# RWKV-5 attention into a cosine router: the order of the lead-in on GpSimd and ScalarE, of the embeddings' transposes, and of the first early transposes

## The chip, the cores and the metric

The kernel runs on one core of a Trainium2 chip. The metric is the time of one execution on the device in microseconds (us), as a median over several executions. Engines are named as in the profile: PE is TensorE's matrix unit, PEld its weight loads, DVE VectorE, ACT ScalarE, POOL GpSimd, SP the SyncE queue that issues most DMAs.

## What is computed

The reference chains two blocks. The first is an RWKV-5 linear attention over 4 batches, 8 heads, 768 steps and 48 channels per head. The second routes each of the 3072 resulting rows of 384 numbers to one of 8 experts by a cosine score, and applies that expert.

```python
for t in range(S):                                     # attention, per batch b and head h
    cur = einsum('bhd,bhe->bhde', u * k[t], v[t])
    y[t] = einsum('bhd,bhde->bhe', r[t], state + cur)
    state = w * state + einsum('bhd,bhe->bhde', k[t], v[t])
x = y.transpose(0, 2, 1, 3).reshape(3072, 384)
logits = normalised(x) @ normalised(expert_emb).T / tau
expert = argmax(logits); gate = softmax(logits)[expert]
out[row] = gate * (relu(x[row] @ w1[expert]) @ w2[expert])
```

## The kernel before

Everything is fp32. Attention is done in chunks of 128 steps: 6 chunks by 4 batches make 24 units, and unit n is chunk n // 4 of batch n % 4. After it come the experts, one after the other, sorted by how many rows they got. No scheduler moves anything: on every engine the instructions stand in the order in which the Python code issues them, and each engine works through its own queue in that order. Order in the code is therefore the subject of this case.

**What a unit needs.** The keys `K` and receptances `R` of a unit are loaded as 128 steps by 8 heads by 48 channels. `scaled` (L317) multiplies K by `kpow`, powers of the decay w, into one of four padded tiles `Kpad`. `turn_r` (L360, L362) transposes R on PE and multiplies it by the decay powers `rpow` into `RT`. `turn_k` (L369, L378) transposes Kpad on PE into the PSUM tile `kt` and copies it on ACT into `KT`. `scores` (L388) multiplies KT by RT into two PSUM tiles `at`; `masked` (L394) applies the triangular mask on DVE, into `AT0` and `AT1`. `sums` (L443, L452) multiplies the old state and the values V by these into `y`, copied on ACT to `yT` (L457). `states` (L409) computes what the chunk adds to the state, `carry` (L422 to L425) adds it. The term with u is taken apart: `own_k` and `own_r` (L328, L332, both on POOL) make u·k·r in the tile `KU`, `own_sum` (L337) adds it up on DVE into `diag`, and `own_rows` (L346) multiplies V by it on ACT into `xd`. `rows` (L470, L476) transposes yT back on PE and adds xd on DVE into the rows `X`. `turn_rows` (L556, L558) transposes X once more, into the PSUM tile `xp` and, by an ACT copy, into `xT`, which the router's logits (`logits`, L572) use.

**The loop.** `attention` runs i from -1 to 23. An iteration turns R and K of unit i + 1, prepares on POOL Kpad, KU of unit i + 2, finishes `sums` and `states` of unit i, makes scores and masks of unit i + 1, rows of unit i, and the transposes of the rows of unit i - 1. Small steps of the router, of the constants' tables (`build_turned`, L197 to L213) and of the expert embeddings (`build_experts`) are put in between. The embeddings are scaled on ACT (L248), transposed on PE (L252) and copied on DVE into `ent` (L253).

**The lead-in.** `build_first` comes before the loop. It loads unit 0, has DVE make the powers of w (L89 to L95), ACT `rpow` (L98) and then eight small casts of constants (`cast`, L126), transposes `kp` on PE into the PSUM tile `kpT` (L107), and copies that on DVE into `kpow` (L110). Unit 0's own Kpad is multiplied in place from the same PSUM tile (L112). On POOL `own(k, 0)`, that is L328 and then L332, stands before the first `scaled` of the loop, which is unit 1's.

**The way into the experts.** In unit 22 the two least filled experts are already known, and one tile of rows for each is gathered by an indirect DMA (`Early`, L1010). Each has a `turn()` (L1021 on PE into the PSUM tile `early_x`, L1023 on ACT into `earlyx`) and 16 steps on PE, eight `early_h` (L1032) and eight `early_y` (L1041). Behind the loop these steps are dealt out by `fill(n)` between the last routing steps.

**PSUM tiles** are given out by tag from fixed banks in turn. Tag `tp` has banks 0 and 1 and serves rt, yrows, lgT, rank, lists and early_x; tag `xp` has the one bank 7 and serves kpT, xp and the embeddings' ps; tag `st` has bank 6. A tile of a tag waits until the earlier one in that bank has been read.

Of the kernel before, what the change touches and what calls it, by code (L numbers as in the profile page):

```python
# [48 lines left out]
def build_first(k):  # L49


    nc, pool = k.nc, k.aconst
    wc = pool.tile([128, NP], F32, name="wc")
    nc.vector.memset(wc, 1.0)
    with nc.allow_non_contiguous_dma(reason="384 words"):
        for s, q in ((0, nc.sync), (1, nc.scalar)):
            q.dma_start(out=wc[s * DP : s * DP + D, :], in_=k.w.rearrange("(p s) d -> s d p", s=2)[s])
    k.ones = k.const.tile([128, 128], F32, name="ones")
    nc.vector.memset(k.ones, 1.0)
    wide = k.work.tile([128, 512], F32, name="wide", tag="AT1")  # L60
    nc.vector.memset(wide, 1.0)
    k.ident = k.const.tile([128, 128], F32, name="ident")
    make_identity(nc, k.ident)

    def busy(columns):
        ps = k.ps.tile([128, 512], F32, name="wake", tag="y")
        nc.tensor.matmul(ps[:, 0:columns], k.ones, wide[:, 0:columns], start=True, stop=True)

    for _ in range(WAKE):
        busy(512)  # L70
    k.Kpad, k.Rpad = (
        [pool.tile([128, H, DP], F32, name=f"{name}{i}") for i in range(count)]
        for name, count in (("Kpad", 4), ("Rpad", AHEAD + 2))
    )
    pads = k.Kpad + k.Rpad
    for t in pads:
        nc.gpsimd.memset(t[:, :, D:DP], 0.0)
    load(k, 0, k.Kpad[0])
    for i in range(1, AHEAD - 1):
        load(k, i)  # L80
    load_rows(k)


    nc.gpsimd.tensor_scalar(wc, wc, W_MIN, W_MAX, ALU.max, ALU.min)
    build_numbers(k)
    own(k, 0)
    t = pool.tile([128, NP, C], F32, name="wpow")
    for p in range(NP):
        nc.vector.tensor_tensor_scan(  # L89
            t[:, p, :], wc[:, p : p + 1].to_broadcast([128, C]), k.ones, 1.0, ALU.mult, ALU.mult  # L90
        )
    mid = pool.tile([128, NP], F32, name="mid")
    nc.vector.reciprocal(mid, t[:, :, C // 2])
    kp = k.work.tile([128, NP, C], F32, name="kp", tag="AT0")
    nc.vector.tensor_mul(kp, t[:, :, ::-1], mid[:, :, None].to_broadcast([128, NP, C]))  # L95
    k.rpow = pool.tile([128, NP, C], F32, name="rpow")
    for p in range(NP):
        nc.scalar.mul(k.rpow[:, p, :], t[:, p, :], mid[:, p : p + 1])  # L98
    cast(k)

    kt = turned_k(k, 0)
    k.KT[0] = k.work.tile([128, NP, C], F32, name="KT", tag="KT")
    nc.vector.tensor_mul(k.KT[0], kt, kp)
    turn_r(k, 0)
    ps = k.ps.tile([128, NP, 2, DP], F32, name="kpT", tag="xp")
    for p in range(NP):
        nc.tensor.transpose(ps[:, p].rearrange("q s d -> q (s d)"), kp[:, p, :], k.ident)  # L107
    busy(192)
    k.kpow = pool.tile([128, H, D], F32, name="kpow")
    nc.vector.tensor_copy(k.kpow.rearrange("q (p s) d -> q p s d", s=2), ps[:, :, :, 0:D])  # L110
    first = k.Kpad[0].rearrange("q (p s) d -> q p s d", s=2)[:, :, :, 0:D]
    nc.vector.tensor_mul(first, first, ps[:, :, :, 0:D])  # L112
    k.wC = t[:, :, C - 1 : C].to_broadcast([128, NP, D])
# [10 lines left out]
def cast(k):  # L124
    for f, i in k.casts:
        k.nc.scalar.copy(f, i)  # L126
    k.casts.clear()
# [192 lines left out]
def own(k, i):  # L320

    own_k(k, i)
    own_r(k, i)
# [68 lines left out]
def masked(k, i, s):  # L392
    a = k.work.tile([128, NP, C], F32, name=f"AT{s}", tag=f"AT{s}")
    k.nc.vector.tensor_mul(a, k.at[i][s], k.umask[:, None, :].to_broadcast([128, NP, C]))  # L394
    k.AT.setdefault(i, []).append(a)
# [451 lines left out]
def attention(k):  # L847


    units = B * NCH  # L850

    def on(f, i, *more):
        if 0 <= i < units:
            f(k, i, *more)

    def of_group(f, i):
        if 0 <= i < units:
            f(k, k.groups[i // B], i % B)

    def whole(f, i, *more):  # L860
        if 0 <= i < units and i % B == B - 1:
            f(k, k.groups[i // B], *more)

    emb, tables = build_experts(k), build_turned(k)
    for i in range(-1, units):
        j = i - SETTLED * B
        if 0 < i + AHEAD < units:
            load(k, i + AHEAD)
        whole(places, i - 4)
        whole(logits_out, i - 3)  # L870
        if i >= 0:
            on(turn_r, i + 1)
        if i == 0:
            own_sum(k, i)
        if B <= i < units - 1:
            on(own_rows, i, 0)
        if i >= 0:
            on(turn_k, i + 1)
        if 0 < i < B:
            own_rows(k, i, 0)  # L880
        whole(turn_logits, i - 3)
        if i == B + 3:
            norms(k, k.groups[0])
        on(scaled, i + 2)
        on(own, i + 2)
        for n in SQUARES.get(i, (i - 1,)):
            of_group(squares, n)
        if B <= i < units - 1:
            on(own_rows, i, 1)
        if i > B + 1:  # L890
            whole(norms, i - 2)
        if j == 10:
            k.lists = turned_lists(k, perm, "tp")
            lists = taken_by_rank(k, k.lists)
            first = [Early(k, r, *lists, w) for r, w in zip(LAST, k.weights)]
        whole(choose, i - 3)
        whole(before, i - 3)
        whole(located, i - 4)
        whole(gates, i - 5)
        whole(lanes, i - 5)  # L900
        whole(listed, i - 5)
        if 0 <= i < units - 2:
            on(own_sum, i + 1)
        if i == B:
            next(emb)
        if j == 7:
            load_, count = loads(k, "xp")
        if j == 9:
            expert_of(k, by)
            number = expert_number(k, LAST[0])  # L910
            load_w1(k, number, k.weights[0][0])
        on(sums, i)
        on(states, i)
        for n in (0, 1) if i == 0 else (1,) if 0 < i < B else ():
            own_rows(k, i, n)
        whole(taken, i - 6, "xp")
        whole(exps, i - 4)
        on(carry, i)
        if 0 < i < B + 2:
            next(tables)  # L920
        whole(summed, i - 6)
        on(scores, i + 1)
        on(masked, i + 1, 0)
        if i == 0:
            masked(k, i + 1, 1)
        on(rows, i)
        if i != 0:
            on(masked, i + 1, 1)
        if i == units - 2:
            own_sum(k, i + 1)  # L930
            own_rows_once(k, i + 1)
        of_group(put, i)
        if j == 10:
            load_w2(k, number, k.weights[0][1])
        of_group(turn_rows, i - 1)
        whole(logits, i - 2)
        whole(ranks, i - 3)
        if i == 0:
            build_constants(k)
        if i in (1, 2, 3):  # L940
            next(emb)
        if 3 <= i < 3 + len(k.ring):
            k.nc.gpsimd.memset(k.ring[i - 3], 0.0)
        if j == 8:
            by = order(k, load_)
        if j == 9:
            settle(k, by, count)
            perm = turner(k, by)


    g, h = k.groups[NCH - 2], k.groups[NCH - 1]
    early = itertools.chain(*(f.steps(lambda: to) for f in first))

    def fill(count):
        for _ in range(count):
            next(early, None)

    load_weights(k, expert_number(k, LAST[1]), k.weights[1])
    first[0].turn()
    gates(k, g)  # L960
    lanes(k, g)
    listed(k, g)
    turn_rows(k, h, B - 1)
    first[1].turn()
    squares(k, h, B - 1)
    norms(k, h)
    fill(1)
    logits(k, h)
    logits_out(k, h)
    fill(1)  # L970
    turn_logits(k, h)
    choose(k, h)
    before(k, h)
    to = outs(k, lists[0], E * TM)
    taken(k, g, "tp")
    fill(2)
    ranks(k, h)
    load_, _ = loads(k, "xp")
    places(k, h)
    exps(k, h)  # L980
    located(k, h)
    lanes(k, h)
    gates(k, h)
    listed(k, h)
    summed(k, g)
    by = order(k, load_, k.settled)
    perm = turner(k, by)
    fill(6)
    taken(k, h, "tp")
    summed(k, h)  # L990
    fill(1)
    lists = turned_lists(k, perm, "xp")
    k.take, k.gates = taken_by_rank(k, lists)
    k.rows_of = {r: gathers(k, r) for r in LAST}
    k.to = outs(k, k.take, E * TM)
    caps_passed(k, load_, by)
    for _ in early:
        pass
# [615 lines left out]
```

## Time and profile before

| What | us |
|---|---|
| median of 6 runs (lowest, highest) | 400.19 (400.1, 400.63) |
| the profiled execution | 400.13 |
| its span, first to last instruction | 398.0 |
| busy in the span: PE, PEld | 387.6, 352.5 |
| busy in the span: DVE, ACT, POOL | 254.4, 172.7, 161.6 |
| mean granted TensorE clock | 0.995 |

The profiled execution took 400.13 us, of which 2.13 lie outside the span. A row of the timeline is: start in us, busy us, engine, source line, operation, output and inputs, shapes, count of instructions, and in brackets the engine's idle time just before with what ended it. Several instructions of one kind that follow each other are one row. A matmul of fp32 data counts twice, a transpose once.

### The profile page before, as it was taken

To read this page: it belongs to the slowest core of one execution; us is meant where nothing else is said; L and a number is where in the kernel's file an instruction comes from. 1 tells how busy PE (TensorE), PEld (TensorE's weight loads), DVE (VectorE), ACT (ScalarE), POOL (GpSimd) and SP (SyncE) were. 2 spreads that over 40 slices of the span, in tenths; PEclk is the share of its full clock that TensorE was granted. 3 is DMA by queue.
4 is the path that set the end of the run, shared out by engine and by line. 5 is a ranking of instruction groups with operands and counts; after the bars stand their busy time and mean duration, and the time that the engine had idled before them with its cause. 6 is when DMAs were issued, how large, how long until landed. Compare 5 with 4: busy or idle time off the path is not lost.

```text
span 398.0 us, 9267 instructions
## 1 busy us (share of the span) xinstructions
PE 387.6 (97%) x3542; PEld 352.5 (89%) x3542; DVE 254.4 (64%) x601; ACT 172.7 (43%) x523; POOL 161.6 (41%) x216
## 2 busy tenths in 40 slices
PE   7999999999999999999999999999999999999993
PEld 4888888888888777899999999999999999899783
DVE  6887888888788770666667668266365556656601
ACT  3787777767677411433233332233233243133020
POOL 7999696867664232500701502220350350300111
PEclk9999999999999999999999999999999999999998
DMA  7999997767615972243705613334164170150111
GB/s 146 177 187 195 195 202 156 151 134 150 135 42 201 310 270 68 87 161 159 254 4 185 231 72 128 104 140 161 45 235 158 43 226 13 40 179 0 40 39 44
DMA packets 93797, 54.35 MB, mean 137 GB/s; under 512 B 76938, under 2 KB 88381, under 8 KB 93747
## 3 DMA queue, kind: packets, MB, share of 16 engines
q1 hardware_dynamic: 90242, 44.26, 40.9%
q0 software_dynamic: 3296, 9.44, 7.3%
q8 instruction: 29, 0.48, 0.5%
q14 instruction: 22, 0.17, 0.1%
q10 hardware_dynamic: 208, 0.00, 0.0%
HBM read 44.45 MB, written 9.63 MB: 136 GB/s over the span
## 4 chain that ended last, share of the span: by engine, by line
PE 91%; ACT 3%; DVE 1%; POOL 1%; DMA 1%; issue 1%; SPq 0%; POOLq 0%; DVEq 0%
PE ps L1222 25%; PE ps L1286 18%; PE ps L1326 5%; PE at L388 5%; PE y L452 5%; PE ps L1340 4%; PE yrows L470 3%; PE early_h L1032 3%; PE early_y L1041 3%; PE ps L1200 3%; PE rt L360 2%; PE ps L1170 2%; PE y L443 2%; PE kt L369 2%; PE st L409 2%; PE xp L556 2%
## 5 line engine op out<-in xcount | busy, mean ns | idle before, releaser
L1086 POOL DMA_INDIRECT out_dram<-y,to x25 | 30.5, 1221 | 173.1 <-DVE Sh L1361 110.0
L1222 PE MATMUL ps<-xTe,w 128*128 128x192 f32 (+3 forms) x336 | 62.9, 327 | 0.0
L1222 PEld LDWEIGHTS ps<-xTe,w 128*128 128x128 f32 x336 | 55.9, 190 | 0.5
L346 ACT ACTIVATE xd<-V,diag 128x48 f32<-128x48 f32 x184 | 46.2, 325 | 0.0
L394 DVE TENSOR_TENSOR AT<-at,umask 128x512 f32<-128x512 f32 x48 | 32.7, 684 | 9.6 <-PE at L388 9.4
L1229 ACT ACTIVATE hT<-hT 128x384 f32<-128x384 f32 (+3 forms) x42 | 22.0, 523 | 32.6 <-DVE hT L1252 16.7
L1286 PE MATMUL ps<-Tw,Sh 128*128 128x192 f32 x192 | 32.5, 326 | 0.0
L1286 PEld LDWEIGHTS ps<-Tw,Sh 128*128 128x128 f32 x192 | 31.4, 190 | 0.0
L1077 POOL DMA_INDIRECT G<-xs,take x25 | 27.0, 1081 | 10.5 <-issue 5.8
L1222 PE MATMUL ps<-Tx,Sw 128*128 128x192 f32 (+3 forms) x168 | 29.7, 326 | 0.0
L388 PE MATMUL at<-RT,KT 48*128 48x128 f32 x384 | 27.9, 285 | 0.3 <-DVE RT L362 0.3
L1239 DVE TENSOR_TENSOR u<-ps,p 128x384 f32<-128x384 f32 (+3 forms) x14 | 7.8, 558 | 31.4 <-ACT p L1236 16.6
L1222 PEld LDWEIGHTS ps<-Tx,Sw 128*128 128x128 f32 x168 | 27.6, 190 | 0.1
L452 PE MATMUL y<-AT,V 128*48 128x128 f32 (+1 forms) x384 | 26.2, 278 | 0.0
L388 PEld LDWEIGHTS at<-RT,KT 48*128 48x128 f32 x384 | 23.3, 187 | 2.6 <-issue 0.9
L332 POOL TENSOR_TENSOR KU<-KU,Rpad 128x384 f32<-128x384 f32 x24 | 24.2, 1007 | 1.9
L452 PEld LDWEIGHTS y<-AT,V 128*48 128x48 f32 (+1 forms) x384 | 19.8, 124 | 4.4 <-issue 3.4
L1286 PE MATMUL ps<-w,hT 128*128 128x192 f32 x128 | 23.4, 326 | 0.0
L328 POOL TENSOR_TENSOR KU<-K,u_bc 128x384 f32<-128x384 f32 x23 | 23.3, 1011 | 0.0
L317 POOL TENSOR_TENSOR Kpad<-K,kpow 128x384 f32<-128x384 f32 x23 | 23.1, 1006 | 0.1
L558 ACT COPY xT<-xp 128x384 f32<-128x384 f32 x24 | 11.5, 479 | 25.1 <-PE xp L556 23.9
L1249 ACT ACTIVATE hT<-ps 128x384 f32<-128x384 f32 (+3 forms) x14 | 6.9, 491 | 35.5 <-PE ps L1222 32.5
(240 smaller groups left out, 817.9 us busy)
## 6 DMA issues: line engine op xcount, KB each, us to landing
w<-in_moe_w_dram SPq DMA_DIRECT2D x16, 1536.0 KB, 7.0
Rpad<-in_r_dram SPq DMA_DIRECT2D x24, 192.0 KB, 5.1
V<-in_v_dram SPq DMA_DIRECT2D x24, 192.0 KB
xs<-X SPq DMA_DIRECT2D x24, 192.0 KB, 3.0
K<-in_k_dram SPq DMA_DIRECT2D x23, 192.0 KB, 3.5
G<-xs,take POOLq DMA_INDIRECT x27
out_dram<-y,to POOLq DMA_INDIRECT x25
Kpad<-in_k_dram SPq DMA_DIRECT2D x1, 192.0 KB
```

What stands on the lines that cost most here:

```text
L317: k.nc.gpsimd.tensor_mul(k.Kpad[i % len(k.Kpad)][:, :, 0:D], k.loaded[i][0], k.kpow)
L328: k.nc.gpsimd.tensor_mul(k.KU[i], k.loaded[i][0], k.u_bc)
L332: k.nc.gpsimd.tensor_mul(k.KU[i], k.KU[i], k.loaded[i][1][:, :, 0:D])
L346: k.nc.scalar.mul(k.xd[i][:, h, :], V[:, h, :], diag[:, h : h + 1])
L388: nc.tensor.matmul(at[s][:, p, :], KT[rows, p, :], RT[rows, p, :], start=True, stop=True)
L394: k.nc.vector.tensor_mul(a, k.at[i][s], k.umask[:, None, :].to_broadcast([128, NP, C]))
L452: mm(y[s][u * DP : u * DP + n, q, :], V[:, h * D : h * D + n], AT[s][:, p, :], start=(c == 0 and q == 0), stop=True, skip_group_check=True,)
L1077: nc.gpsimd.indirect_dma_start(out=G[0:n, :], out_offset=None, in_=k.xs[:, :], in_offset=IndirectOffsetOnAxis(ap=take[0:n], axis=0), bound ...
L1086: put = k.nc.gpsimd.indirect_dma_start(out=k.out[:, :], out_offset=IndirectOffsetOnAxis(ap=to, axis=0), in_=y, in_offset=None, bounds_chec ...
L1222: nc.tensor.matmul(ps[:, j, :], weights[:, (f + j) * 128 : (f + j + 1) * 128], moving, start=(first and j == 0), stop=True, skip_group_che ...
L1229: nc.scalar.activation(h, h, ACT.Relu)
L1286: nc.tensor.matmul(ps, a[:, f, :], b[:, f, :], start=(first and f == 0), stop=(f == NF // 2 - 1), skip_group_check=True)
```

## The change

Five edits in three places. In the lead-in, `own(k, 0)` is cut in two: `own_k` stays in `build_first`, and `own_r` of unit 0 moves into the loop's first iteration, behind `scaled` of unit 1. The copy of kpT into `kpow` goes from DVE to ACT, in front of the eight casts, which were in front of the transposes. In iteration 4 the last step of the embeddings (three transposes on PE and the copy into `ent` on DVE) moves from in front of `sums` to behind `states`, `carry`, a step of the tables and `summed`. At the end of attention, the first expert's `turn()` moves from behind the loop to in front of `rows` of unit 23; the second one's takes the place of the first, and is followed by a `fill(1)` that is new there.

```diff
@@ build_first
     build_numbers(k)
-    own(k, 0)
+    own_k(k, 0)
...
         nc.scalar.mul(k.rpow[:, p, :], t[:, p, :], mid[:, p : p + 1])
-    cast(k)
...
     k.kpow = pool.tile([128, H, D], F32, name="kpow")
-    nc.vector.tensor_copy(k.kpow.rearrange("q (p s) d -> q p s d", s=2), ps[:, :, :, 0:D])
+    nc.scalar.copy(k.kpow.rearrange("q (p s) d -> q p s d", s=2), ps[:, :, :, 0:D])
+    cast(k)
@@ attention, in the loop
         on(scaled, i + 2)
+        if i < 0:
+            own_r(k, 0)
         on(own, i + 2)
...
-        if i == B:
-            next(emb)
...
         whole(summed, i - 6)
+        if i == B:
+            next(emb)
         on(scores, i + 1)
         on(masked, i + 1, 0)
         if i == 0:
             masked(k, i + 1, 1)
+        if i == units - 1:
+            first[0].turn()
         on(rows, i)
@@ attention, behind the loop
     load_weights(k, expert_number(k, LAST[1]), k.weights[1])
-    first[0].turn()
+    first[1].turn()
+    fill(1)
     gates(k, g)
     lanes(k, g)
     listed(k, g)
     turn_rows(k, h, B - 1)
-    first[1].turn()
     squares(k, h, B - 1)
     norms(k, h)
     fill(1)
```

## The prediction

> **What bounds the kernel now.** I read the page first: PE is busy nearly throughout, so time is won only where PE waits.
>
> ```profile
> PE 387.6 (97%) x3542; PEld 352.5 (89%) x3542; DVE 254.4 (64%) x601; ACT 172.7 (43%) x523; POOL 161.6 (41%) x216
> ```
>
> Then the view of waits, for PE over the whole span. Its columns are the total, the number of times and the longest.
>
> ```profile
> PE kt L369 <- POOL Kpad L317: 0.6, 1, 0.6
> PE rt L360 <- DMA Rpad<-in_r_dram: 0.4, 1, 0.4
> PE xp L556 <- ACT xT L558: 0.4, 1, 0.4
> ...
> PE ps L252 <- ACT emb L248: 0.2, 1, 0.2
> PE yrows L470 <- ACT yT L457: 0.2, 1, 0.2
> ```
>
> The three places of the change are three of these waits: 0.6 for unit 1's kt, 0.2 for the embeddings, 0.2 + 0.4 at the last rows. Together that is 1.2 us, 0.3% of the time, so each must be followed in the timeline. The lead-in first, then the landing of unit 1's K (the view of DMA issues around 4 us; the last column is us from issue to landing):
>
> ```profile
> 7.15 1.00 POOL L328 TENSOR_TENSOR KU<-Kpad,u_bc 128x384 f32<-128x384 f32 x1 [1.59 <-DMA u_bc<-in_u_dram]
> 7.32 0.55 DVE L110 COPY kpow<-kpT 128x384 f32<-128x384 f32 x1
> ...
> 8.23 1.00 POOL L332 TENSOR_TENSOR KU<-KU,Rpad 128x384 f32<-128x384 f32 x1
> ...
> 9.05 0.63 PE L360 MATMUL rt<-ident,Rpad 128*128 128x128 f32 x4 [0.44 <-DMA Rpad<-in_r_dram]
> 9.19 1.00 POOL L317 TENSOR_TENSOR Kpad<-K,kpow 128x384 f32<-128x384 f32 x1
> ...
> 10.24 0.66 PE L369 MATMUL kt<-ident,Kpad 128*128 128x128 f32 x4 [0.56 <-POOL Kpad L317]
> ```
>
> ```profile
> K<-in_k_dram SPq DMA_DIRECT2D x1, 192.0 KB, 4.6
> ```
>
> Unit 1's Kpad stands on POOL behind KU's second multiplication, which nobody needs before DVE's diag at 10.45. Its inputs are there early: K, issued at 3.29, landed at 3.29 + 4.6 = 7.89, and kpow was ready at 7.87.
>
> **The lead-in, term by term.** POOL: L328 ends at 8.15, so Kpad runs from 8.19 to 9.19 and KU's L332 after it, to 10.19. The same three operations fill the same stretch, so POOL is where it was from 10.14 on. diag still finds its KU at 10.45.
>
> kpow: DVE loses 0.55. ACT gains a copy of 128x384 from PSUM, the shape of xT, whose row at 18.32 says 0.48. kpT is complete at 6.21 + 0.60 = 6.81 and ACT's rpow ends at 6.60, so kpow is there at about 7.35 and Kpad's start at 8.19 has 0.8 to spare. The eight casts slide from 6.50 to 7.34 and end at about 8.4. Behind them stands ACT's KT copy, which waited 3.33 for PE, so the 0.84 is hidden; without that cover it would cost just that. DVE's free time is worth nothing: its next step, L112, waits until 8.18 for L328 to have read Kpad.
>
> PE: rt stays at 9.05, held by its load. A kt that need not wait starts 0.15 before the rt row ends (13.82 + 0.60 against 14.27), so unit 1's starts at 9.68 - 0.15 = 9.53 with Kpad done at 9.19: 0.71 earlier. It also takes 0.60 instead of 0.66, which makes 0.77 at most. I take 0.74. Next in PE's queue is unit 0's `y`, now at about 10.08. Its masks end at 9.31 and 9.93. V's landing is not in these rows; K landed at 7.89 and R by 9.05, one load in some 1.1, so I estimate V at 10.0 to 10.2, and what it may cost at 0 to 0.1.
>
> **Does the 0.74 pass on?** PE runs without a gap from 10.82 to 27.7, so it does unless another engine, which has not moved, comes to stand in the way. POOL is such a one: its rows follow each other without idle time from 7.15 to 35.20. Cover left after PE moves up by 0.74 (row minus what it needs):
> - kt of units 2, 3, 4 behind Kpad: 13.53 - 13.18, 17.82 - 17.43, 22.12 - 21.97 = 0.35, 0.39, 0.15.
> - RT of unit 2: DVE waits for POOL's KU until 12.26, so its copy of the state stays at 12.73 and the masks behind it move by only 0.43, from 13.48 to 13.05. RT ends at 15.83 - 0.43 = 15.40; the scores want it at 16.26 - 0.74 = 15.52. Cover 0.12.
> - diag of units 3 and 4 (19.82, 24.23) can move by only 0.3 and 0.15, as KU ends at 19.49 and 24.03. The masks behind diag 3 have more cover than that. Unit 4's, finished at 28.11, are wanted by the second half of `y` at about 28.1 after the shift and the move of the embeddings; should PE stand there a little, the wait for ACT below covers it.
>
> The covers are thin but all positive. In iteration 4 the lead passes to ACT:
>
> ```profile
> 25.25 1.20 DVE L206 TENSOR_SCALAR mask<-number,own 128x8 f32<-128x8 f32 x1
> ...
> 26.92 0.48 ACT L558 COPY xT<-xp 128x384 f32<-128x384 f32 x1 [0.44 <-PE xp L556]
> ...
> 31.11 0.61 ACT L457 COPY yT<-y 112x256 f32<-112x256 f32 x2
> 31.50 0.46 PEld L470 LDWEIGHTS yrows<-ident,yT 112*128 112x128 f32 x4 [0.26 <-ACT yT L457]
> ```
>
> ACT works without a gap from xT at 26.92 to yT at 31.11, and yrows waits for it. But that stretch begins with a wait for PE's xp, so it moves up with PE. From 36.6 on PE is bound again and the rest follows it: 0.74 at the end.
>
> The mask row is odd: 1.20 us for 8 columns where the tie of the same shape (L213, at 35.85) took 0.17. It ended at 26.45, with POOL's KU (25.42 to 26.43). DVE now meets an unmoved POOL at other moments, so such a hold can come or go; by this row it is worth up to 1.03 of DVE. The scores are masked from 26.37 on, after it, and the covers above leave room even for an unmoved mask, so I count 0, between 0 and 0.2.
>
> [...]
>
> **The embeddings.** Three transposes (0.35) with their wait (0.20) leave the place before unit 4's `y` and go behind its states; ent (0.17 on DVE) goes with them. PE reaches `y` about 0.5 earlier, but the yrows that follow at 31.50 wait for ACT's queue, not for y (done at 29.90). Moved up, the transposes still fit before them: the next scores end at 31.43 in the old order. ent is wanted by lgT at 37.57, and the next xp at 32.02 shares its bank, both far off. Value 0, bounds +0.3 (the transposes in front of the scores, uncovered) and -0.2 (their wait gone).
>
> **The last rows.** All times here are before the 0.74.
>
> ```profile
> 132.09 0.41 PE L470 MATMUL yrows<-ident,yT 112*128 112x112 f32 x2 [0.19 <-ACT yT L457]
> ...
> 132.66 0.49 PE L1021 MATMUL early_x<-ident,G 128*128 128x128 f32 x3
> ...
> 132.92 0.23 ACT L646 ACTIVATE l<-l 128x32 f32<-128x32 f32 x1 [0.89 <-DVE l L645]
> 133.06 0.46 ACT L558 COPY xT<-xp 128x384 f32<-128x384 f32 x1
> ...
> 133.57 0.55 PE L556 MATMUL xp<-ident,X 128*128 128x128 f32 x3 [0.42 <-ACT xT L558]
> ```
>
> early_x in front of yrows fills the 0.19. The 0.42 looks open to filling too, but its cause stays. ACT stands at the exp until 132.92, for DVE. In the old order the copy after it frees bank 7 for xp. In the new one earlyx's copy comes first, and PE's next step is the second early_x, which needs that bank of tag `tp` back: yrows sits in the other. So PE again goes on at about 133.57, having done the same work. From there both orders hold the same set up to the logits' transpose, one early_h moved. The xp that follows now comes at about 134.7, behind an xT copy that ends at 134.0; lgT's fourth matmul wants the last xT at 135.8, which is ready at 135.7. Value 0, bounds -0.6 (both waits gone) and +0.2.
>
> The new `fill(1)` puts the routing chain one early_h (0.77, from 134.28 to 135.05) later; the gathers at 145.98 to 150.00 feed PE only at 158.79. No DMA moves in SP's or POOL's queue.
>
> **Sum.** The profiled execution is 398.0 of span and 2.13 around it: 400.13 - 0.74 = 399.39, against a median before of 400.19. I say 399.4. A measurement of this kernel can tell about 0.2%, 0.80 us, from no change; the border, 399.39, runs through my forecast.
>
> **Rivals.**
> - *POOL holds the units back.* For it: the covers of 0.12 and 0.15. Against it: they are positive. If one cover is short by 0.4, 0.3 remains: 399.8. Chance 0.13.
> - *Nothing comes of it*: K lands later than 9.2 in the new order, or ACT's stretch from 26.92 does not move up. K's 7.89 and ACT's wait for xp speak against it. 400.1, chance 0.05.
> - *The pauses at the last rows go as well*: 0.74 + 0.61 = 1.35, so 398.8. For it: PE's order is freer. Against it: the shared bank. Chance 0.14.
> - *Slower: early_x waits for its gather.* PE works in order, so with early_x in front, yrows, xp and the routing stand behind the gather's landing. The gather is issued by 127.92; packets of its queue still run between 131.5 and 132.0, and PE asks at 131.56. ACT takes the result only at 133.06, so early_x, 0.49 long, may start as late as 132.5 for nothing; beyond that each us costs one, and 1.3 later than now it decides the sign. Behind a 1536 KB load, at the 390 GB/s of 125 to 129 us some 3.9, it would be 400.13 - 0.74 + 3.4 = 402.8. Against it: the next such load is issued at 130.79, after the gather. Chance 0.08.
>
> **Chances and range.** Forecast 0.60 (399.2 to 399.6, of which 0.36 past the border), with rivals: faster 0.36 + 0.14 = 0.50, same 0.24 + 0.13 + 0.05 = 0.42, slower 0.08. The range 398.9 to 400.1 holds the forecast, the lesser gain and most of the greater one.
>
> **What would show it.** kt of unit 1 without a wait, at about 9.5; scores of unit 1 at 11.55, of unit 5 at or before 29.5, yrows of unit 4 at about 30.8 still behind ACT; a PE pause that ends at about 132.8, now in front of the second early_x and named after ACT's earlyx. A wait of kt or of the scores between 12 and 25 us, or a long wait of the first early_x, would show me wrong.

## The result

The changed kernel took 399.29 us (median of 19 runs, 398.9 to 399.76), the kernel before 400.14 (39 runs): a ratio of 0.9977, with a 95% interval of 0.9971 to 0.9983. The change gains 0.85 us; 0.74 was forecast. The profiled execution took 399.77, as long as the longest of them, and this matters below: its span of 397.7 is only 0.3 shorter than that of before, and the missing 0.5 was lost at one place. Most executions seem to pass it without loss: of the 21 spans on record 17 lie between 397.0 and 397.3. In the experiments below some executions, 10 of the 35 of before in the first group and none of a kernel with POOL's new order, ran at a mean clock of 0.991 to 0.992 and took about 2 us more; the medians given there are over the others, the ratios and intervals over all.

In the code after the change, lines 100 to 110 stand one line earlier (the copy of kpT is L109), and the early expert's are L1025 (early_x), L1027 (earlyx), L1036 (early_h), L1041 (earlyh) and L1045 (early_y).

The page of the kernel after, busy time, and the longest entries of its view of waits for PE (total, times, longest):

```profile
PE 387.4 (97%) x3542; PEld 352.4 (89%) x3542; DVE 254.3 (64%) x600; ACT 173.4 (44%) x524; POOL 161.7 (41%) x216
...
PE early_x L1025 <- ACT earlyx L1027: 0.4, 1, 0.4
PE rt L360 <- DVE AT L394: 0.4, 1, 0.4
...
PE early_x L1025 <- DMA G<-xs,take: 0.3, 1, 0.3
```

PE does the same work. The waits that the change aimed at are gone: kt for Kpad (0.6), the embeddings' ps for ACT (0.2), yrows (0.2) and xp (0.4); that is 1.4 us in all, where the prediction's first paragraph added them up to 1.2. Three others have come. Two of them belong to the last rows. The third, rt waiting for a mask `AT`, was not there before.

The lead-in, in the timeline of the kernel after:

```profile
7.03 0.48 ACT L109 COPY kpow<-kpT 128x384 f32<-128x384 f32 x1 [0.40 <-PE kpT L106]
...
8.32 1.00 POOL L317 TENSOR_TENSOR Kpad<-K,kpow 128x384 f32<-128x384 f32 x1
9.27 1.02 POOL L332 TENSOR_TENSOR KU<-KU,Rpad 128x384 f32<-128x384 f32 x1
...
9.49 0.60 PE L369 MATMUL kt<-ident,Kpad 128*128 128x128 f32 x4
10.02 1.09 PE L452 MATMUL y<-AT,V 128*64 128x128 f32 x16
```

kt of unit 1 has no bracket any more and starts at 9.49 where it started at 10.24: 0.75 earlier. `y` follows without a wait for V. From here PE runs 0.80 and then 0.77 ahead of the profile before; the transposes of unit 4 at 22 us leave 0.66 of it, and this stays up to 37 us. The scores of unit 1 start at 11.49, those of unit 5 at 29.55, yrows of unit 4 at 30.84.

At 38 us most of the lead goes. The stretch in the kernel before:

```profile
35.85 0.17 DVE L213 TENSOR_SCALAR tie<-number 128x8 f32<-128x8 f32 x1
35.91 0.52 POOL L425 TENSOR_TENSOR state<-state,wpow 112x192 f32<-112x192 f32 x1 [0.71 <-DVE state L424]
...
38.36 0.65 PE L360 MATMUL rt<-ident,Rpad 128*128 128x128 f32 x4
```

The same stretch of the kernel after, first DVE and PE, then POOL:

```profile
35.24 2.84 DVE L213 TENSOR_SCALAR tie<-number 128x8 f32<-128x8 f32 x1
35.88 2.20 DVE L394 TENSOR_TENSOR AT<-at,umask 128x512 f32<-128x512 f32 x1
36.76 1.32 DVE L476 TENSOR_TENSOR X<-yrows,xd 128x384 f32<-128x384 f32 x1
...
38.19 0.66 PE L360 MATMUL rt<-ident,Rpad 128*128 128x128 f32 x4 [0.41 <-DVE AT L394]
```

```profile
35.25 0.52 POOL L425 TENSOR_TENSOR state<-state,wpow 112x192 f32<-112x192 f32 x1
35.72 0.41 POOL L947 MEMSET G<- 128x384 f32 x1
36.09 1.00 POOL L317 TENSOR_TENSOR Kpad<-K,kpow 128x384 f32<-128x384 f32 x1
37.05 1.00 POOL L328 TENSOR_TENSOR KU<-K,u_bc 128x384 f32<-128x384 f32 x1
```

`tie` multiplies eight numbers per partition. It took 0.17 before. Here it starts 0.01 before a POOL operation and ends at 38.08, as the fourth POOL operation in a row ends at 38.05. The mask multiplication behind it and the addition into X (L476) stand until then as well. rt of unit 7 waits for DVE: the view names the mask, and by the PSUM tags rt takes the bank of yrows, which L476 has to read first. It starts 0.18 ahead of before, where PE had been 0.66 ahead: a loss of 0.48 in this execution.

The last rows, in the timeline of the kernel after:

```profile
131.69 0.52 PE L1025 MATMUL early_x<-ident,G 128*128 128x128 f32 x3 [0.34 <-DMA G<-xs,take]
132.04 0.55 PE L470 MATMUL yrows<-ident,yT 112*128 112x112 f32 x4
132.43 0.49 PE L556 MATMUL xp<-ident,X 128*128 128x128 f32 x3
132.72 0.23 ACT L646 ACTIVATE l<-l 128x32 f32<-128x32 f32 x1 [0.89 <-DVE l L645]
132.85 0.46 ACT L1027 COPY earlyx<-early_x 128x384 f32<-128x384 f32 x1
...
133.37 0.55 PE L1025 MATMUL early_x<-ident,G 128*128 128x128 f32 x3 [0.45 <-ACT earlyx L1027]
```

A wait of 0.34 for the gather stands where the 0.19 for yT was, and the pause of 0.42 is now one of 0.45 in front of the second early_x. The first early_x ended at 132.21; its copy on ACT stands behind the exp, and the exp behind DVE's `l`. PE's lead is 0.21 on either side of these rows.

One more difference lies behind the places of the change, in the second early expert. First the kernel before, then after; `earlyh` is ACT's relu of `early_h`, in two halves:

```profile
153.20 1.32 ACT L1037 ACTIVATE earlyh<-early_h 128x512 f32<-128x512 f32 x2 [4.00 <-remote]
153.85 0.30 PEld L1041 LDWEIGHTS early_y<-w,earlyh 128*128 128x128 f32 x2 [0.16 <-ACT earlyh L1037]
```

```profile
152.20 0.60 ACT L1041 ACTIVATE earlyh<-early_h 128x512 f32<-128x512 f32 x1 [3.20 <-PE early_h L1036]
```

Before, ACT took the first half up only at 153.20, and PE's early_y stood for it; after, it took it up at 152.20, in time. PE's lead grows here from 0.21 to 0.44, and 0.45 is left at PE's last matmul. What held ACT is not shown: "remote" means that the profile has no releaser. The same late start stands in three other profiles with the old order of the last rows, swap_only, kpow_only and emb_only, but not in before_exp; with the new order it stands in tie_and_exp alone.

### The profile page after: what moved, and what is told of

It is laid out like the page before. It is cut to its first block, busy times and chain, and to the rows that moved or that the text cites. A ratio compares the mean times of both kernels' runs of the same rounds, so it can differ in the third digit from the quotient of the medians.

```text
span 397.7 us, 9266 instructions
## 1 busy us (share of the span) xinstructions
PE 387.4 (97%) x3542; PEld 352.4 (89%) x3542; DVE 254.3 (64%) x600; ACT 173.4 (44%) x524; POOL 161.7 (41%) x216
## 4 chain that ended last, share of the span: by engine, by line
PE 92%; ACT 2%; DVE 2%; DMA 1%; issue 1%; SPq 1%; POOL 0%; POOLq 0%; DVEq 0%; ACTq 0%
PE ps L1226 25%; PE ps L1290 18%; PE at L388 5%; PE y L452 5%; PE ps L1330 5%; PE ps L1344 4%; PE yrows L470 3%; PE early_h L1036 3%; PE rt L360 3%; PE early_y L1045 3%; PE ps L1204 3%; PE y L443 2%; PE ps L1174 2%; PE kt L369 2%; PE st L409 2%; PE xp L556 2%
## 5 line engine op out<-in xcount | busy, mean ns | idle before, releaser
L394 DVE TENSOR_TENSOR AT<-at,umask 128x512 f32<-128x512 f32 x48 | 33.6, 720 | 9.1 <-PE at L388 8.9
L328 POOL TENSOR_TENSOR KU<-K,u_bc 128x384 f32<-128x384 f32 x23 | 23.2, 1009 | 0.0
```

What stands on the lines that cost most here:

```text
L328: k.nc.gpsimd.tensor_mul(k.KU[i], k.loaded[i][0], k.u_bc)
```

## The experiments

Three groups of four kernels, each group on one chip with the kernel before beside it. The profiles differ in the lead-in (POOL's first wait, for u_bc, ended 0.6 to 0.8 later in the first group's than in that of before), so times are compared within a group.

**First group: the parts one by one.** The kernel before took 400.85.

`swap_only`, POOL's order alone:

```diff
     build_numbers(k)
-    own(k, 0)
+    own_k(k, 0)
...
         on(scaled, i + 2)
+        if i < 0:
+            own_r(k, 0)
```

> The kernel before with only GpSimd's swap: own_r(0) behind scaled(1); kpow stays on VectorE and the casts stay where they were. The whole change gave -0.85 us. Theory A (the lead-in's swap is the gain): kpow was ready at 7.87 in the profile of before, ahead of the 8.3 at which GpSimd can start Kpad, so the copy's engine does not matter: kt of unit 1 starts at about 9.5 without a wait and the time is 0.65 to 0.85 below before. Rival B (the move of kpow to ScalarE is what lets Kpad start early): kt comes later than 9.7 and under 0.4 is gained. Rival C (the gain is made at the last rows): kt at 9.5, but the time is within 0.3 of before.

Measured: 400.14, 0.71 less; ratio 0.9965 (0.9949 to 0.998). The timeline of swap_only, and behind it the same rows of emb_only, which has the old lead-in on the same chip:

```profile
8.94 1.01 POOL L317 TENSOR_TENSOR Kpad<-K,kpow 128x384 f32<-128x384 f32 x1
9.99 0.66 PE L369 MATMUL kt<-ident,Kpad 128*128 128x128 f32 x4
```

```profile
9.99 1.00 POOL L317 TENSOR_TENSOR Kpad<-K,kpow 128x384 f32<-128x384 f32 x1
11.04 0.66 PE L369 MATMUL kt<-ident,Kpad 128*128 128x128 f32 x4 [0.79 <-POOL Kpad L317]
```

Kpad follows L328 (7.98 + 1.00) at once, though kpow is still copied by DVE, and kt comes 1.05 earlier. Not all of it lasts: 0.86 is left behind unit 4's kt, and the spans differ by 0.8 (398.9 and 398.1). Theory A holds. (kt came at 9.99, later than Theory A's 9.5 and Rival B's 9.7, which were set by the loads in the profile of before; against the old order on the same chip the reading is plain.)

`kpow_only`, the copy and the casts alone:

```diff
-    cast(k)
...
-    nc.vector.tensor_copy(k.kpow.rearrange(...), ps[:, :, :, 0:D])
+    nc.scalar.copy(k.kpow.rearrange(...), ps[:, :, :, 0:D])
+    cast(k)
```

> The kernel before with only kpow's copy moved to ScalarE and the eight casts behind it; GpSimd's order stays. Theory A: Kpad still stands behind KU's second multiplication, kt of unit 1 stays at 10.2, the time is within 0.15 of before. Rival B: at least 0.3 is gained.

Measured: 400.91, 0.06 more; ratio 1.0002 (0.9984 to 1.002). kt waits 0.55 for Kpad, as before. Rival B falls: this move alone is worth nothing, and swap_only needed no part of it.

`emb_only`, the embeddings alone:

```diff
-        if i == B:
-            next(emb)
...
         whole(summed, i - 6)
+        if i == B:
+            next(emb)
```

> The kernel before with only the embeddings' step moved behind the states of unit 4. Theory A: PE's 0.2 wait in front of the embeddings' transposes goes, yrows at 31.5 still waits for ScalarE's yT, so the time is within 0.15 of before. Rival: the transposes stand bare in front of the scores (0.2 to 0.3 slower), or the wait is a true gain (0.2 faster).

Measured: 400.89, 0.04 more; ratio 1.0004 (0.9985 to 1.0023). The wait of ps for ACT is gone from PE's list, that of yrows for yT (0.2) is still in it.

`last_only`, the last rows alone:

```diff
+        if i == units - 1:
+            first[0].turn()
         on(rows, i)
...
-    first[0].turn()
+    first[1].turn()
+    fill(1)
...
-    first[1].turn()
```

> The kernel before with only the last edit: first[0].turn() in front of the last rows, first[1].turn() and one step of the early expert in its place. Theory A: one pause of about 0.45 stays (the second early_x behind ScalarE's copy, which stands behind the exp), a wait for the gather of 0.1 to 0.4 takes the place of the 0.19; 0 to 0.25 faster. Rival C: both pauses go and 0.5 to 0.7 is gained.

Measured: 400.72, 0.13 less; ratio 0.9976 (0.9959 to 0.9992). PE's waits of last_only at this place, by its own line numbers:

```profile
PE early_x L1023 <- ACT earlyx L1025: 0.5, 1, 0.5
PE early_x L1023 <- DMA G<-xs,take: 0.3, 1, 0.3
```

Both are there without the new lead-in. The old pauses have not gone, they have been renamed; Rival C falls. Against the profile of before PE stands where it stood on both sides of the pauses (0.62 behind), and gains 0.23 further on, where the second expert's early_y no longer waits for earlyh. So the 0.13, if it is more than noise, was not made at the pauses. The four parts sum to 0.71 - 0.06 - 0.04 + 0.13 = 0.74; the whole gave 0.85 on its chip. Over all executions the sum would be 1.0, so that it meets the forecast to two digits is chance.

**Second group: the hold on DVE and the pause behind the exp.** The kernel before took 401.01.

`after_again`, the changed kernel once more:

> The changed kernel itself once more, so that the three kernels of this call have it beside them on one chip, and for a second profile of it. In its first profile VectorE's tie (128x8, 0.17 before) stood for 2.84, from 35.24 to 38.08, while four GpSimd operations followed each other without idle time, and PE's lead over before fell from 0.72 to 0.18 there. If that hold follows from the two engines' positions, tie is held for more than 1 us again; if it is a matter of chance, it comes out anywhere between 0.17 and 2.9. Time 0.7 to 1.0 below before.

Measured: 399.83 (399.69 to 400.35), 1.18 less than before; ratio 0.9955 (0.9938 to 0.9972), more than was expected. The profiled execution is again the longest of its runs, 400.35, and again `tie` is held. The timelines of after_again and of exp_later, whose instructions are the same up to this point:

```profile
35.87 2.82 DVE L213 TENSOR_SCALAR tie<-number 128x8 f32<-128x8 f32 x1
```

```profile
35.61 0.56 DVE L213 TENSOR_SCALAR tie<-number 128x8 f32<-128x8 f32 x1
```

So the code alone does not decide, nor does the chip. Over the six profiles that have both the swap and tie on DVE it took 2.84, 2.82, 0.56 (three times) and 0.16; with POOL's old order 0.16 or 0.17 (before, emb_only, last_only, before_exp). What goes with it can be read from the starts: in all five held rows tie and POOL's L425 begin within 0.01 of each other; in the five free ones it began 0.06 ahead of it (in the old order because POOL had waited some 0.7 for DVE's state). That tells held from free; why the hold lasted for one POOL operation in three profiles and for four in two, the starts do not tell.

`tie_on_act`, the eight numbers written by ScalarE:

```diff
-    nc.vector.tensor_scalar(k.tie, k.number, N + 1.0 / 16, None, ALU.mult)
+    nc.scalar.mul(k.tie, k.number, N + 1.0 / 16)
```

> The changed kernel with tie (128x8) written by ScalarE instead of VectorE; nothing else moves. Theory P (the small VectorE operation is held behind GpSimd's chain, and the mask multiplication behind it makes PE's rt wait): rt of unit 7 no longer waits for AT, the lead of 0.7 to 0.8 passes 38 us whole, and the time is 0.2 to 0.5 below after_again. Rival Q (the AT step waits for GpSimd or PE for another reason, or the next small operation is held in its place): the lead at 39 us is again under 0.4 and the time is within 0.15 of after_again.

Measured: 399.79 (399.51 to 400.03), 0.04 below after_again; ratio to before 0.9956 (0.994 to 0.9972). In its profile rt of unit 7 has no wait and starts at 38.05, against 38.79 in after_again: 0.25 of that it was already ahead from 15 us on, 0.49 is the hold. This profile alone would not prove theory P, since in exp_later rt has no wait either with tie on DVE; the rows of the two held executions do show its chain. The price in time is Rival Q's. Both are true together if only a part of the executions is held. That the two longest were is what the two profiles show; the spans hint at the others: 4 of after_again's 10 lie at 398.0 to 398.3, all 9 of tie_on_act at 397.6 to 397.9.

`exp_later`, the exp of group 4 behind the first early_x's copy (`scaled_logits` is `exps` without its last instruction, the exp, and `exp_only` is that):

```diff
-        whole(exps, i - 4)
+        whole(exps if i < units - 1 else scaled_logits, i - 4)
...
         if i == units - 1:
             first[0].turn()
+            whole(exp_only, i - 4)
```

> The changed kernel with ScalarE's last exp (128x32) issued behind earlyx's copy instead of in front of it. Theory E (the pause of 0.45 in front of the second early_x is ScalarE standing at the exp for VectorE's l): the pause goes, and the time is 0.3 to 0.45 below after_again. Rival F (another wait takes its place: xT's copy, the bank, the routing): PE's pause comes a little later and less than 0.15 is gained.

Measured: 399.14 (398.96 to 399.31), 0.69 below after_again; ratio to before 0.9935 (0.9913 to 0.9957). The timeline of exp_later, where early_x is L1037 and its copy L1039:

```profile
131.55 0.52 PE L1037 MATMUL early_x<-ident,G 128*128 128x128 f32 x3 [0.32 <-DMA G<-xs,take]
...
132.16 0.48 ACT L1039 COPY earlyx<-early_x 128x384 f32<-128x384 f32 x1 [0.46 <-PE early_x L1037]
132.60 0.23 ACT L657 ACTIVATE l<-l 128x32 f32<-128x32 f32 x1
132.69 0.55 PE L1037 MATMUL early_x<-ident,G 128*128 128x128 f32 x3
```

The copy starts when early_x ends, the exp behind it loses nothing, and the second early_x has no wait. PE's lead over after_again grows here by 0.48 and stays to the end. Theory E holds for the changed order. The 0.2 beyond it is not explained; held executions of after_again may be in it.

`tie_and_exp`, both edits:

> Both edits on the changed kernel. Theories P and E: the gains add, 0.5 to 0.9 below after_again, which is 1.3 to 1.8 below before. Rivals Q and F: within 0.2 of after_again.

Measured: 399.36 (399.19 to 400.4), 0.47 below after_again and 0.22 above exp_later; ratio to before 0.9945 (0.9924 to 0.9966). The gains did not add. Its profiled execution, the longest, waits 0.6 at 154.0, early_y for ACT's earlyh: the late start of ACT seen before, and longer. PE loses 0.88 there. Why ACT was late, and whether this holds the median back, stays open.

**Third group: the same pause in the old order, a better order, and a late gather.** The kernel before took 399.89.

`before_exp`, the exp moved in the kernel before:

```diff
-        whole(exps, i - 4)
+        whole(exps if i < units - 1 else scaled_logits, i - 4)
...
         of_group(turn_rows, i - 1)
+        if i == units - 1:
+            whole(exp_only, i - 4)
```

> The kernel before with only the last exp moved: ScalarE's exp (128x32) behind xT's copy instead of in front of it. Theory E (the exp is the cause of the pause in both orders): PE's wait of 0.42 in front of the last xp goes, the 0.19 for yT stays, and the time is 0.25 to 0.45 below before. Rival F: the next wait takes its place and under 0.15 is gained.

Measured: 399.83, 0.06 less; ratio 1.0005 (0.9993 to 1.0017). A miss of the 0.25 to 0.45; Rival F's "under 0.15" is met. The timeline of before_exp:

```profile
132.46 0.49 PE L556 MATMUL xp<-ident,X 128*128 128x128 f32 x3
...
132.99 0.48 ACT L558 COPY xT<-xp 128x384 f32<-128x384 f32 x1 [0.83 <-PE xp L556]
...
133.53 0.55 PE L556 MATMUL xp<-ident,X 128*128 128x128 f32 x3 [0.24 <-ACT xT L558]
```

The pause shrinks from 0.42 to 0.24 only. In the old order the copy waits for its own xp, which ends at 132.95, and the next xp needs the one bank of that tag; the exp had added only some 0.2. In the new order early_x ended 0.6 before its copy could start, and there the exp was the whole pause.

`exp_xp`, exp_later with the earlier row's xp in front of the first early_x:

```diff
         if i == units - 1:
+            of_group(turn_rows, i - 1)
             first[0].turn()
             whole(exp_only, i - 4)
...
-        of_group(turn_rows, i - 1)
+        if i < units - 1:
+            of_group(turn_rows, i - 1)
```

> exp_later, and the row before's xp (three transposes of X) moved in front of the first early_x, so that PE has work while the gather lands. The gather's wait of 0.3 in front of the first early_x shrinks to under 0.1, and earlyx's copy, now behind xT's on ScalarE, comes just in time for the second early_x: 0.15 to 0.3 below exp_later, some 0.6 to 0.9 below the changed kernel. If X or the bank is not free there, or earlyx's copy comes late, the wait only moves and the time is that of exp_later, 0.4 to 0.7 below the changed kernel.

Measured: 398.65 (398.47 to 398.77), 1.24 below before; ratio 0.9969 (0.9957 to 0.9981). The timeline of exp_xp (early_x L1039, its copy L1041):

```profile
130.63 0.55 PE L556 MATMUL xp<-ident,X 128*128 128x128 f32 x3
131.01 0.50 PE L1039 MATMUL early_x<-ident,G 128*128 128x128 f32 x3
131.35 0.55 PE L470 MATMUL yrows<-ident,yT 112*128 112x112 f32 x4
...
132.14 0.55 PE L1039 MATMUL early_x<-ident,G 128*128 128x128 f32 x3 [0.24 <-ACT earlyx L1041]
```

The gather's wait is gone: xp fills it. 0.24 comes back in front of the second early_x, since ACT now copies xT first. From the last `y` to the second early_x exp_xp gains 0.57 on the changed kernel's first profile (PE's lead grows from 0.65 to 1.22), and exp_later 0.55 (from 0.12 to 0.67), so the fill brings next to nothing where 0.15 to 0.3 was expected. With exp_xp_tie it has the lowest time; exp_later, on another chip, was not timed beside it.

`exp_xp_tie`, with tie on ScalarE as in tie_on_act:

> exp_xp with tie written by ScalarE. The hold of tie on VectorE is a matter of chance that most executions of the changed kernel do not meet, so the median stays within 0.15 of exp_xp; only the highest of the runs comes closer to the median.

Measured: 398.56 (398.4 to 398.78), 0.09 below exp_xp; ratio to before 0.9965 (0.9952 to 0.9979). As expected, except that the range is not narrower.

`late_gather`, the early rows' gathers at the start of the next iteration (the removed line stood at j == 10):

```diff
+        if j == 11:
+            first = [Early(k, r, *lists, w) for r, w in zip(LAST, k.weights)]
...
-            first = [Early(k, r, *lists, w) for r, w in zip(LAST, k.weights)]
```

> The changed kernel with the two gathers of the early rows issued one iteration later, behind GpSimd's xd: about 132.1 instead of 126.4 for the first. It prices the slower rival: PE works in order, so the first early_x and all behind it wait. If each us that the gather lands after 131.7 costs PE one, the time rises by as much as the wait in front of the first early_x grows from its 0.34: 3 to 6 us, to 402 to 405. If yrows, xp and the routing could run past it, or the time were made good later, it would rise by less than half of the wait.

Measured: 406.86 (406.68 to 408.03); ratio 1.0172 (1.0157 to 1.0188). The timeline, and the windows of late_gather (stretch and its length, busy of PE, PEld, DVE, ACT, POOL, granted clock, DMA share, GB/s):

```profile
137.94 0.87 PE L1026 MATMUL early_x<-ident,G 128*128 128x128 f32 x3 [6.88 <-DMA G<-xs,take]
```

```profile
126.00:131.00 5.00, 5.00 (x83) 4.22 (x75) 4.22 (x18) 2.89 (x12) 0.38 (x1) 1.00 0.71 265
131.00:138.00 7.00, 0.12 (x3) 0.10 (x2) 0.99 (x5) 0.70 (x3) 2.77 (x3) 0.65 0.87 282
138.00:142.00 4.00, 4.00 (x20) 4.00 (x21) 1.78 (x6) 1.43 (x3) 0.41 (x2) 0.50 0.15 53
142.00:146.00 4.00, 4.00 (x49) 3.42 (x47) 0.37 (x2) 1.26 (x4) 1.38 (x2) 0.82 0.82 281
```

The wait grows by 6.88 - 0.34 = 6.54, and nothing gets past it. But the span, 406.0, is 8.3 above the changed kernel's 397.7: after the pause PE runs at a granted clock of 0.50, and early_x takes 0.87 instead of 0.52. The work from the first early_x to lgT takes 143.73 - 137.94 = 5.79 instead of 135.51 - 131.69 = 3.82, although the pause of 0.45 in front of the second early_x is gone. By the spans a us of waiting costs 8.3 / 6.54 = 1.27; by the medians, with 0.85 for the change, (406.86 - 399.89 + 0.85) / 6.54 = 1.2. The second is a rough estimate: the 0.85 is from another chip, and the wait is that of the longest execution. It was expected to cost one, and the gather to land 3 to 6 us late, so 402 to 405 was missed twice.

## Why the prediction was right, and where it was not

**The lead-in** went as worked out. POOL's swap was taken as 0.74; kt moved by 0.75 (to 9.49, forecast 9.53), y to 10.02 (10.08), and the swap alone gave 0.71. V cost nothing. That the median moved by 0.85 is in part luck, as the account at the end of this section shows. kpow on ACT was put at nothing: its copy ended at 7.51 ahead of Kpad's 8.32, the casts slid beside ACT's wait, and kpow_only gave no gain.

**It passes on**, with thin covers, and two gave way a little: the scores of unit 2, with a cover of 0.12, lower the lead from 0.80 to 0.77, and unit 4's kt, with a cover of 0.15, to 0.66. POOL had started 0.1 late from 10.24 on because u_bc landed late. The rival of POOL holding the units back was right in kind, and its 0.4 was too much: 0.14 went. The scores of unit 5, forecast at or before 29.5, came at 29.55.

**The step that failed is the hold on DVE.** It was counted "0, between 0 and 0.2" from the mask row alone. The mask was held longer, 1.65 instead of 1.20, and cost nothing, as argued. But `tie`, named in that very paragraph as the one that took 0.17, now met POOL: before, POOL had 0.71 of idle time there; afterwards DVE had moved up by 0.6 and POOL worked through. The two profiled executions so held lost 0.48 and 0.49, more than the bound of 0.2. The median, which the forecast is about, does not show it (0.04 between after_again and tie_on_act).

In both rows tie ends 0.03 after a POOL operation does (38.08 against 38.05 in after, 38.69 against 38.66 in after_again). From the mask row the prediction took such a hold to be worth up to 1.03 of DVE; these rows stood through four POOL operations, 2.84 and 2.82 where before took 0.17. Even so both executions, 399.77 and 400.35, were faster than the median of before beside them, 400.14 and 401.01.

**The embeddings** were put at 0 and gave -0.04. **The last rows** were put at 0 within -0.6 and +0.2. last_only gave a gain of 0.13, but not at the pauses: the second early_x was to stay where the pause of before ended, and with the lead of 0.2 it did (133.37 against 133.57). But the cause was named too simply. The prediction said of both orders that ACT stands at the exp; in before_exp's profile the pause of the old one is 0.24 without the exp in its way, so the exp was less than half of the 0.42, and the single bank with its copy the rest. The slower rival did not come: the gather landed at 131.69, ahead of the point (132.5 less the lead) from which it was to cost. Its price was put at one for one; late_gather gives about 1.2 to 1.3, as behind its pause of 6.88 the clock of 0.50 came on top.

**The sum** was 0.74 from one term, and the profiles of before and after give another account: 0.66 of the lead-in lasts, the embeddings and the last rows give about 0, early_y's wait for ACT's late earlyh gives 0.23, which the prediction did not name, the hold takes 0.48 in the profiled execution, and 0.1 goes behind PE's last matmul. That makes the 0.35 between the two spans, and 0.83 without the hold, near the median's 0.85. Whether ACT is late in most executions of before is not known, so the 0.23 is read from single executions. That the whole gave 1.18 on another chip may come from the lead-in, which differs from profile to profile: kt's wait for Kpad was 0.56 in before's, and 0.55 to 0.9 in the four experiments with the old POOL order. That was not tested by itself.

## What to carry to other kernels

In a kernel bound by one engine working in order, list the waits of that engine, and for each ask what its releaser stood behind: here one swap of two queue entries on GpSimd and one exp moved behind a copy on ScalarE gave most of what was found. Do not file a pause under the engine that stands at it; undo the suspected cause in both orders, since nearly the same pause had two causes. Follow the lead of the bounding engine through the whole trace and not only at the places that the change names: here 0.23 came from elsewhere. When an edit moves two engines against each other, look for the small VectorE operations in the stretches where GpSimd has just lost its idle time (here 0.71 of it, and tie went from 0.17 to 2.84), and do not take one profile's time for the median's.

## What the runs showed of the hardware

A VectorE operation on 128x8 numbers, tie, that took 0.17 us in before stood for 2.84 in after and 2.82 in after_again while four GpSimd operations ran back to back, for 0.56, to within 0.04 of the end of the first of them, in swap_only, exp_later and exp_xp, which also have GpSimd's new order, and took 0.16 in late_gather, which has it too. In the five held cases it began within 0.01 of a GpSimd operation, in the free ones 0.06 ahead of it: a few hundredths of a us go with being held or free. What sets one operation or four is open.

In late_gather's pause of 6.88 us the granted clock fell to 0.50 at 133.17, 2.1 us after PE's last matmul (its mean is 0.65 from 131 to 138 and 0.50 from 138 to 142), and was full again at 143.41, 5.5 us after PE had restarted (0.82 from 142 to 146). At the start of the kernel the traces of before and after record the full clock from 5.12 and 5.07 on, 3.4 and 3.3 us after the first matmul at 1.73. In late_gather's profile the transposes kt, from 5.31, took 1.06 where they took 0.60 in these two, rt, from 6.16, 0.96 instead of 0.63, and kpT, from 6.95, 0.60 as there.
